# State-space outputs parked in one transfer a block, tokens in the order 8t+m, and a replanned order of work

## The chip, the cores and the metric

The kernel runs on one core of a Trainium2 chip. A core has engines that run on their own and meet at semaphores: TensorE (PE in the profile) multiplies matrices into PSUM, VectorE (DVE) and ScalarE (ACT) work on SBUF and PSUM, GpSimd (POOL) on SBUF, and SyncE (SP) issues most of the transfers. The metric is device time in microseconds, the median over runs; the kernel before has 750.5 us (three runs, 749.81 to 752.56).

## The reference

Two branches over the same 2048 tokens of 512 channels are mixed by a gate of the token:

```python
g = sigmoid((x * gate_w).sum(-1, keepdims=True))
a = softmax_attention(x, wqkv, 32 heads of 16) @ wo       # full 2048 x 2048 scores
# state-space branch, channel d, 128 complex states n:
K = einsum("dn,dnl,dn->dl", C, exp(dt * A * l), dt * B).real   # a filter of 2048 taps
b = causal_convolution(u, K).astype(bf16) + u * Dskip
out = g * a + (1 - g) * b
```

The attention has 32 heads with scores of 2048 by 2048 each, so 134 million exponentials. The state-space branch first makes the filters K from powers of complex numbers, then convolves each channel with its own filter.

## The kernel before, in words

**Attention.** The scores come in 2048 tiles. A tile is 128 keys by 512 queries of one head; four tiles (one for each 32-row strip of PE's array) make a quad, sixteen quads (all keys) a block, and there are 32 blocks, ordered by query chunk, then by heads. Tiles are put into groups of three (683 groups), each with a bank set SC0 or SC1 in PSUM by turns. For group g, PE computes the scores (`qk`, line 757 by way of the helper `mm`), ACT takes the exponential into a ring of tiles (`ex`, line 1018), and later PE multiplies the ring's tiles with the values (`pv`) into OA. The ring has NS = 14 tiles (named ET in the profile), from group NSG = 335 on NS2 = 24 (the rest is named EX).

**Sets.** ACT is relieved by DVE: in some groups ACT does only two tiles, and DVE turns the third into the bits of an exponential (`bits`, line 1040, tile DZ). Four such tiles, one of each strip, make a set; POOL makes three shifted copies of a set (`batch`, line 1059, tile DU), and PE adds all four to OA (`sums`). `decide` forms the sets as it hands out the tiles. A set begins only if fewer sets exist than the curve PACE allows at this group (`due`), only in certain key tiles of a block (DVK, and STRX, STRE, STRK for the last three), not within four groups of the last set, and if DVE has a reserve in the plan. WIN gives the number of buffers: two DZ and four DU up to group 560, then four and six.

**State-space branch.** `bases` and `tables` make powers on DVE (buffers Z, B16, T), `kstage` contracts them on PE into MB and writes filters to memory, `yloads` brings filters (H) and shifted inputs (U), `ystage` convolves on PE (MB) and multiplies with 1-g (gt) on DVE into Yst (line 1593). `yout` (line 1601) parks Yst in memory, four transfers a block of 32 channels, and loads it back with tokens on partitions (Yl, Yl2; line 1612). `outs` projects the attention with Wo, adds Yl and stores rows (fo).

**Gate.** `gate` (line 1620) makes the logits on PE, turns them by a trip through memory (gld to gp), takes an exponential on ACT (line 1638), three small DVE steps, and spreads g and 1-g by 14 small transfers (gt, gq).

**The order of the work** is written by a planner at build time. Each helper thread yields pieces with an engine and an estimated cost; between two groups, `Sched.fill` issues those that can start before a time limit (t+OVER), by earliest start and priority. `Prog` keeps a model clock of each engine. Each engine runs its queue strictly in that order, so a piece that waits holds back all behind it. If a group would lack matmul work (FILL up to group 260, then LOW), filler matmuls on a zero tile (wm) are added. DVE and POOL steps that would share a port are kept apart by waits (`locks`). SBUF addresses follow from each buffer's first and last use (`place`), and a buffer that takes over another's bytes waits for its users.

Of the kernel before, what the change touches and what calls it, by code (L numbers as in the profile page):

```python
# [56 lines left out]
NS = 14  # L57
NS2 = 24
NSG = 335
# [7 lines left out]
YLP = 4.5  # L67
YQ = 0
XGO = 'g14'
YGO = 'projs'  # L70
YLGO = 'K15'
BG0 = 'g0'
BG1 = 'g0'
BG2 = 'K4'
BG3 = 'g0'
TP = 2
KP = 0.4
NB = 2
NT = 2
TB = 0  # L80
# [4 lines left out]
HS = [4, 48, 8]  # L85
BACK = 0.4
# [17 lines left out]
DVCAP = 6  # L104
DVK = 14
JS = ((2, 0, 3, 1), (1, 0, 2, 3), (0, 2, 1, 3))
DVL = 16
STRX = 480
# [3 lines left out]
VG = 4 * VW + 16  # L112
ONES = struct.unpack("<f", bytes.fromhex("803f803f"))[0]
# [285 lines left out]
class Sched:  # L399
# [101 lines left out]
    def fill(self, until, pe_until, want=0):  # L501
        while True:
            best = None
            for t in self.thr:
# [3 lines left out]
                if t.eng == "PE":  # L508
# [7 lines left out]
                    if e + t.cost + room > pe_until and t.up > 0 or e > min(until, pe_until):  # L516
                        continue
# [35 lines left out]
def declare(nc, es):  # L553
# [188 lines left out]
def record(nc, p, B, ins):  # L742
# [106 lines left out]
    def proj_ev(kind, idx, c, bank):  # L849
        b, off, sl = bank  # L850
        if kind == "K":
            o, at, ky = KT, idx * S + 512 * c, (idx, c)
        elif c + idx:
            o, at, ky = B["Qs"], idx % 2 * 512, idx % 2
        else:
            o, at, ky = B["Q"], 0, 0
        op("DVE", lambda v: v.tensor_copy(o(at, [[1, 512]]), b(off, [[1, 512]])), [(b, sl, ('p', kind, idx, c))],
           [(o, ky)], c=.62)
# [11 lines left out]
    def mk_qm(b, j):  # L870
# [363 lines left out]
    def fp(qr, k, dims, off=0):  # L1234
        return B[f"Z{qr % NZ}"].f32(ZF.get(k[0], 0) + 128 * k[1] + off, dims)

    def fk(qr, *ks):
        return [(B[f"Z{qr % NZ}"], k, qr) for k in ks]

    PS = 2048  # L1240

    def weights(qr):

        Z = B[f"Z{qr % NZ}"]
# [109 lines left out]
    def zpart(qr):  # L1354

        Z = B[f"Z{qr % NZ}"]
# [43 lines left out]
    def ploads():  # L1400
        yield ("AFTER", "pd")
        for qr, go in enumerate((BG0, BG1, BG2, BG3)):
            Z = B[f"Z{qr % NZ}"]
# [11 lines left out]
    def bases():  # L1415
        for qr, go in enumerate((BG0, BG1, BG2, BG3)):
            yield ("AFTER", go)
            B16 = B[f"B16{qr % NB}"]
# [121 lines left out]
    def yloads():  # L1540
        yield ("AFTER", YGO)
        for v in range(2 * NBLK):
# [4 lines left out]
            for i in range(UN4):  # L1547
# [3 lines left out]
                    [(xs, (v // 8, s0)) for s0 in range(0, T, 4)], [(U, i, v)], c=.62, lat=3.5, b=UB * 2 / UN4, pace=True)  # L1551
            for q in range(4):
# [5 lines left out]
                for i in range(HN):  # L1558
# [3 lines left out]
                        [(kd, (u // 8, u // 2 % 4))], [(H, i, u)], c=.6, lat=3.5, b=HB / HN, pace=True)  # L1562
# [38 lines left out]
    def yout(blk):  # L1601
        w = blk % 2
        for j in range(4):
            yield ("SP", .6)
            dma("SP", lambda e, j=j: e.dma_start(yd.dram(512 * blk + 128 * j, [[8192, 2 * T], [8192 * 2 * T, R8], [1, 128]]),
                                                 Yst(1024 * w, [[128, R8], [1, 128]], 32 * j, 2 * T)),
                [(Yst, (w, h), blk) for h in range(2)], [(yd, (blk, j))], c=.6, lat=3.5, b=YB)
        yield ("AFTER", YLGO)
        for k, y in enumerate((Yl, Yl2)):
            yield ("SP", .6, YLP)  # L1610
            n = 128 >> k
            dma("SP", lambda e, k=k, y=y, n=n: e.dma_start(y(4 * n * blk, [[n, 4], [1, n]]), yd.dram(512 * blk + 8192 * k, [[8192 * 2, P], [128, 4], [1, n]])),
                [(yd, (blk, j)) for j in range(4)], [(y, blk)], c=.6, lat=3, b=.5, pace=True)
# [5 lines left out]
    def gate():  # L1619
# [16 lines left out]
        dma("SP", lambda e: e.dma_start(gp(0, [[1, 16]]), B["gld"].dram(0, [[16, P], [1, 16]])), [(B["gld"], c) for c in range(4)], key("gp"), c=.6, lat=2.5)  # L1636
# [10 lines left out]
        for j in range(4):  # L1647
            yield ("SP", .6)
            dma("SP", lambda e, j=j: e.dma_start(alt("gt", [[16, R8], [1, 16]], 32 * j), B["gd"].dram(0, [[16, T], [16 * T, R8], [1, 16]])),
                [(B["gd"], 0)], [(B["gt"], j)], c=.6, lat=2.5)  # L1650
            yield ("SP", .6)
            dma("SP", lambda e, j=j: e.dma_start(alt("gt", [[16, R8], [1, 8]], 32 * j + 1), B["gd"].dram(8, [[16, T], [16 * T, R8], [1, 8]])),
# [25 lines left out]
    def out_dma(lt, q="SP"):  # L1678
        dma(q, lambda e: e.dma_start(dap(ins["out"], 128 * lt * D, [[D, P], [1, D]]), fo((lt % 4) * D, [[1, D]])),
# [121 lines left out]
    def norms():  # L1801
        for b in range(31):
# [84 lines left out]
    op("DVE", lambda v: v.tensor_scalar(Qm(0, [[1, 512]]), OA(0, [[1, 512]]), msk(0, [[1, 1]]), None, ALU.mult),  # L1887
# [25 lines left out]
    for g in range(NG):  # L1913
# [114 lines left out]
```

## Time and profile before

| | us |
|---|---|
| median of the three runs | 750.5 |
| the profiled execution, its own time | 751.56 |
| span, first to last instruction | 749.8 |
| ACT busy | 729.4 |
| PE busy | 688.2 |
| DVE busy | 661.7 |
| POOL busy | 368.3 |

The profile is of one execution. A busy share is an average over stages that differ: before about 200 us DVE makes projections and filter parameters and takes no score tiles; from 200 to 630 us sets, filters and convolutions run side by side; after that the sets and the output projection. A row of the profile names the line, engine, operation, tiles and shapes, then the count, busy time and mean time, then the idle time of the engine just before and who ended it. Lines of helpers (757 for all matmuls, 1112 for many DVE steps) are told apart by their tiles.

### The profile page before, as it was taken

The page shows a single profiled execution, that of the slowest core. Times are in us where ns is not written, and L with a number is a line of the kernel's source. Part 1 is how long each engine was busy: PE and PEld are TensorE (multiplying, and loading weights), DVE is VectorE, ACT ScalarE, POOL GpSimd, SP SyncE. Part 2 cuts the span into 40 slices and gives each one's busy share as a digit, 9 for nine tenths or more (in the row PEclk, how much of TensorE's full clock was granted, in tenths as well). Part 3 has the DMA queues.
Part 4 walks back from the last instruction along what each step waited for, and adds up shares of the span by engine and source line. Part 5 has one row for each costly group of instructions (what it writes and reads, how often), then busy time and mean ns, then how long its engine had stood idle before and what let it go on. Part 6 is the DMA issues. An engine that isn't in the chain of part 4 may idle for free.

```text
span 749.8 us, 31499 instructions
## 1 busy us (share of the span) xinstructions
PE 688.2 (92%) x13936; PEld 290.6 (39%) x13936; DVE 661.7 (88%) x1113; ACT 729.4 (97%) x696; POOL 368.3 (49%) x368
## 2 busy tenths in 40 slices
PE   8777777888899999999999999999999999999997
PEld 4222232443434344434454344544444443222222
DVE  7999899999889888988989879999888888898876
ACT  7999999999999999999999989999999999999996
POOL 3000000000056777564453645467788788878763
PEclk9999999999999999999999999999999999999999
DMA  9858920221556457767268787737577774100000
GB/s 218 164 149 145 164 49 6 60 51 64 126 137 173 118 138 171 200 156 206 58 153 216 173 231 210 190 79 166 155 171 165 173 167 84 30 18 20 26 23 29
DMA packets 176588, 94.33 MB, mean 126 GB/s; under 512 B 116802, under 2 KB 159940, under 8 KB 176452
## 3 DMA queue, kind: packets, MB, share of 16 engines
q1 hardware_dynamic: 175492, 91.48, 50.8%
q8 instruction: 109, 1.79, 1.0%
q10 hardware_dynamic: 960, 0.85, 0.4%
q14 instruction: 27, 0.22, 0.1%
HBM read 63.42 MB, written 18.90 MB: 110 GB/s over the span
## 4 chain that ended last, share of the span: by engine, by line
ACT 77%; PE 17%; DVE 3%; DMA 1%; POOL 1%; issue 0%; DVEq 0%; SPq 0%; POOLq 0%
ACT ET L1018 63%; ACT EX L1018 14%; PE OA L757 7%; PE SC L757 7%; PE MB L757 3%; DVE DZ L1040 1%; POOL DU L1059 1%; DVE ft L1112 1%; DMA gp<-gm_gld 1%; DMA H<-gm_kd 0%; DVE T L1112 0%; DVE OT L1080 0%; DVE Yst L1593 0%; DVE OnT L1104 0%; DVE Qm L1887 0%
## 5 line engine op out<-in xcount | busy, mean ns | idle before, releaser
L1018 ACT ACTIVATE ET<-SC 128x1024 bf16<-128x1024 f32 (+1 forms) x538 | 590.0, 1348 | 8.0 <-PE SC L757 6.4
L1059 POOL INT64_ADD DU<-DZ x348 | 360.9, 1051 | 367.4 <-DVE DZ L1040 251.3
L1040 DVE TENSOR_SCALAR DZ<-SC 128x512 uint16<-128x512 f32 x468 | 312.7, 683 | 59.6 <-PE SC L757 47.9
L757 PE MATMUL SC<-Qm,KT 32*128 32x512 bf16 x2048 | 275.9, 385 | 47.9 <-ACT ET L1018 41.5
L757 PEld LDWEIGHTS SC<-Qm,KT 32*128 32x128 bf16 x2048 | 70.8, 91 | 251.3 <-ACT ET L1018 170.7
L1018 ACT ACTIVATE EX<-SC 128x1024 bf16<-128x1024 f32 (+1 forms) x145 | 148.3, 1236 | 0.7 <-PE SC L757 0.6
L757 PE MATMUL OA<-DU,VE 128*32 128x512 bf16 x1404 | 133.8, 387 | 3.0 <-POOL DU L1059 3.0
L757 PE MATMUL OA<-ET,VE 128*32 128x512 bf16 x1276 | 131.0, 389 | 0.3 <-ACT ET L1018 0.2
L757 PEld LDWEIGHTS MB<-U,H 128*32 128x32 bf16 x4096 | 83.9, 144 | 27.9 <-issue 18.3
L757 PE MATMUL MB<-U,H 128*32 128x128 bf16 (+7 forms) x4096 | 91.6, 225 | 1.3 <-DMA H<-gm_kd 1.0
L757 PE MATMUL OA<-wm 128*32 128x256 bf16 (+3 forms) x317 | 60.0, 344 | 1.2 <-DVE idf L812 1.2
L1112 DVE TENSOR_TENSOR T<-B,DT 128x1536 bf16<-128x1536 bf16 x64 | 60.6, 974 | 0.1
L757 PEld LDWEIGHTS OA<-DU,VE 128*32 128x32 bf16 x1404 | 36.5, 96 | 50.8 <-issue 35.9
L757 PEld LDWEIGHTS OA<-ET,VE 128*32 128x32 bf16 x1276 | 33.5, 95 | 48.9 <-issue 46.7
L757 PEld LDWEIGHTS MB<-T,Z 128*32 128x32 bf16 x2048 | 43.5, 155 | 10.7 <-issue 7.2
L757 PE MATMUL MB<-T,Z 128*32 128x64 bf16 (+1 forms) x2048 | 46.7, 235 | 0.0
L757 PE MATMUL OA<-DZ,VE 128*32 128x512 bf16 x468 | 46.5, 387 | 0.0
L757 PE MATMUL OA<-EX,VE 128*32 128x512 bf16 x304 | 42.8, 388 | 0.0
L1112 DVE TENSOR_TENSOR ft<-Z 128x512 f32<-128x512 f32 (+3 forms) x48 | 39.8, 855 | 0.1
L1112 DVE TENSOR_TENSOR Z<-ft,ft 128x1024 bf16<-128x1024 bf16 (+3 forms) x56 | 32.2, 574 | 0.5
L1080 DVE STREAM_TRANSPOSE OT<-OA 128x512 f32<-128x512 f32 x32 | 22.9, 716 | 2.1 <-PE OA L757 1.9
L1593 DVE TENSOR_TENSOR Yst<-MB,gt 128x512 bf16<-128x512 f32 x32 | 21.8, 682 | 3.3 <-PE MB L757 3.1
(141 smaller groups left out, 416.7 us busy)
## 6 DMA issues: line engine op xcount, KB each, us to landing
H<-gm_kd SPq DMA_DIRECT2D x128, 256.0 KB, 4.1
U<-gm_xs SPq DMA_DIRECT2D x128, 134.2 KB, 3.9
T<-B SPq DMA_DIRECT2D x16, 256.0 KB, 2.7
gm_yd<-Yst SPq DMA_DIRECT2D x64, 64.0 KB, 3.5
gm_kd<-Ks SPq DMA_DIRECT2D x64, 40.0 KB, 1.9
gm_xs<-xP SPq DMA_DIRECT2D x16, 136.0 KB, 5.7
gm_pd<-L SPq DMA_DIRECT2D x8, 256.0 KB, 4.1
Z<-gm_pd SPq DMA_DIRECT2D x8, 256.0 KB, 3.6
```

The lines of the kernel that those rows point to most:

```text
L757: op("PE", lambda t: t.matmul(out(), lhsT(), rhs(), start=start, stop=stop, skip_group_check=True, **kw), R, W, c=c, lat=.15, a=a, cfg=cfg)
L1018: op("ACT", lambda a: a.activation(E(at, [[1, 512 * n]]), sc(0, [[1, 512 * n]]), AF.Exp, scale=DH ** -0.5), [(sc, i, g) for i in range(n)] ...
L1040: op("DVE", lambda v: v.tensor_scalar(z.u16(512 * k, [[1, 512]]), sc(1024, [[1, 512]]), XS, XB, ALU.mult, ALU.add), [(sc, 2, g)], [(z, k, ...
L1059: op("POOL", lambda v, u=u, cut=cut: v.int64_add(u.u64(), z.u64(), cut * 0x0001000100010001), R, [(u, 0, i)], c=1.016, lat=.09, lk=True)
L1080: op("DVE", lambda v: v.transpose(OT(512 * w, [[1, 512]]), OA(0, [[1, 512]])), [(OA, 0, b)], [(OT, w, b)], c=.64)
L1112: op(eng, lambda v: v.tensor_tensor(o(), a(), b_(), f), R, W, c=c)
L1593: op("DVE", lambda v, w=w, h=h: v.tensor_tensor(Yst(1024 * w + 4 * h, [[128, R8], [8, 16], [1, 4]]), MB(0, [[1, R8], [R8, 16], [NC, 4]]), ...
```

## The change: what it does

- *Parking.* `yout` writes a block's Yst in one transfer (partition rows of 1024 elements, 2 KB runs) in place of four (runs of 128 elements, 256 bytes). The load back reads runs of 128 or 64 elements, for Yl in place of one run of 512.
- *Token order.* For this, the tokens of a tile of 128 stand in the order 8t+m (t of 16, m of 8) for token t+16m: the query copies read PSUM with steps of 16 (ROWS, TURNED), the gate's small transfers and the output rows follow the same order.
- *Buffers by quarter.* Z, B16 and T have a name for each quarter of the channels, so that `place` can give them bytes of their own; the flags that release a quarter stay (they use NZ, NB). A quarter's first tables no longer wait for those of the quarter before.
- *Ring.* NS 14 to 20, and 24 tiles from group 395 in place of 335.
- *Gate.* The exponential comes after group 100 (GATE).
- *Sets.* A set may begin only if the last set in its DZ buffer has been through POOL in the plan (`room`); four DZ and six DU buffers from group 480; another PACE curve; last key tiles of a block allowed from group 460.
- *Plan.* Other priorities, costs, start points, limits (OVER by whether the next group is a set's), filler and rest parameters.

The diff, cut:

```diff
-LAZY = 9
-PDEL = 0.3
+LAZY = 5
+PDEL = 0.43
...
-OUTP = 6
-YSEG = 4
+OUTP = 3.78
+YSEG = 2
...
-FILL = 1500
-LOW = 1300
-SURP = 256
+FILL = 1450
+LOW = 1200
+SURP = 192
...
-OVER = 0.5
-REST = (14, 0, 1792, 425)
+OVER = (0.27, 0.64)
+REST = (13, 1, 1792, 425)
...
-NS = 14
+NS = 20
...
-NSG = 335
+NSG = 395
...
-WIN = ((0, 560, 2, 4), (560, 679, 4, 6))
-PACE = ((0, 0), (40, 0), (90, 0), (140, 0), (200, 15.0), (270, 28.3), (340, 39.5), (420, 53.9), (500, 73.9), (570, 90.7), (630, 105.7), (683, 118.95))
+WIN = ((0, 480, 2, 4), (480, 679, 4, 6))
+PACE = ((0, 0), (61, 0), (78, 0.0), (149, 0.0), (206, 12.77), (270, 23.66), (340, 38.94), (414, 52.88), (500, 77.45), (564, 96.69), (630, 111.83), (683, 119.39))
...
-YLGO = 'K15'
-BG0 = 'g0'
-BG1 = 'g0'
-BG2 = 'K4'
-BG3 = 'g0'
-TP = 2
-KP = 0.4
+YLGO = 'K14'
+GATE = 'g100'
+BG0 = 'g25'
+BG1 = 'g20'
+BG2 = 'K3'
+BG3 = 'K3'
+TP = 0.86
+KP = 0.85
...
-HS = [4, 48, 8]
-BACK = 0.4
+HS = [4, 44, 8]
+BACK = 0.66
...
-DVCAP = 6
+DVCAP = 8.7
...
+FREE = 'u{}.2'
...
-STRX = 480
+STRX = 460
...
+ROWS = [[P, 4], [R8, T], [1, R8]]
+TURNED = [[P, 4], [1, T], [T, R8]]
...
-                    if e + t.cost + room > pe_until and t.up > 0 or e > min(until, pe_until):
+                    if e + t.cost + room > pe_until and (t.up > 0 or e > until) or e > pe_until:
...
-    for k in range(NB):
-        sb(f"B16{k}", 2 * 128 * 16)
-    for k in range(NZ):
-        sb(f"Z{k}", 2 * 128 * 32)
-    for k in range(NT):
-        sb(f"T{k}", 14 * 16 * CB)
+    for q in range(4):
+        sb(f"B16{q}", 2 * 128 * 16)
+        sb(f"Z{q}", 2 * 128 * 32)
+        for k in range(NT):
+            sb(f"T{q}{k}", 14 * 16 * CB)
...
-        op("DVE", lambda v: v.tensor_copy(o(at, [[1, 512]]), b(off, [[1, 512]])), [(b, sl, ('p', kind, idx, c))],
+        to, fr = ([[1, 512]],) * 2 if kind == "K" else (ROWS, TURNED)
+        op("DVE", lambda v: v.tensor_copy(o(at, to), b(off, fr)), [(b, sl, ('p', kind, idx, c))],
...
+    def room(w):
+        n = sum(st["w"] == w for st in sets)
+        old = [i for i, st in enumerate(sets) if st["r"] == f"{w}{n % WIN[w][2]}"]
+        return not old or FREE.format(old[-1]) in sch.flag
+
     def win(x):
-        return next((w for w, (lo, hi, *_) in enumerate(WIN) if lo <= x < hi and x >= plan["x"] + 4 and len(sets) < due(x)), None)
+        return next((w for w, (lo, hi, *_) in enumerate(WIN) if lo <= x < hi and x >= plan["x"] + 4 and len(sets) < due(x) and room(w)), None)
...
-                old = [k for k in range(blk) if tbuf(k) == tbuf(blk)]
+                old = [k for k in range(4 * qr, blk) if tbuf(k) == tbuf(blk)]
...
-        for j in range(4):
-            yield ("SP", .6)
-            dma("SP", lambda e, j=j: e.dma_start(yd.dram(512 * blk + 128 * j, [[8192, 2 * T], [8192 * 2 * T, R8], [1, 128]]),
-                                                 Yst(1024 * w, [[128, R8], [1, 128]], 32 * j, 2 * T)),
-                [(Yst, (w, h), blk) for h in range(2)], [(yd, (blk, j))], c=.6, lat=3.5, b=YB)
+        yield ("SP", .6)
+        dma("SP", lambda e: e.dma_start(yd.dram(P * 1024 * blk, [[1024, P // 2], [512 * P, 2], [1, 1024]]), Yst(1024 * w, [[1, 1024]])),
+            [(Yst, (w, h), blk) for h in range(2)], [(yd, blk)], c=.66, lat=3.5, b=2 * YB)
...
-            dma("SP", lambda e, k=k, y=y, n=n: e.dma_start(y(4 * n * blk, [[n, 4], [1, n]]), yd.dram(512 * blk + 8192 * k, [[8192 * 2, P], [128, 4], [1, n]])),
-                [(yd, (blk, j)) for j in range(4)], [(y, blk)], c=.6, lat=3, b=.5, pace=True)
+            dma("SP", lambda e, k=k, y=y, n=n: e.dma_start(y(4 * n * blk, [[n, 4], [1, n]]), yd.dram(P * 1024 * blk + 512 * P * k, [[P, P], [P * P, 4], [1, n]])),
+                [(yd, blk)], [(y, blk)], c=.6, lat=3, b=.55, pace=True)
...
+        yield ("AFTER", GATE)
         yield ("ACT", .3)
...
-        dma(q, lambda e: e.dma_start(dap(ins["out"], 128 * lt * D, [[D, P], [1, D]]), fo((lt % 4) * D, [[1, D]])),
+        dma(q, lambda e: e.dma_start(dap(ins["out"], 128 * lt * D, [[D, T], [T * D, R8], [1, D]]), fo((lt % 4) * D, [[1, D]])),
...
-        sch.fill(t, t + OVER, want)
+        over = OVER[0 if g + 1 in vec else 1]
+        sch.fill(t, t + over, want)
```

Further constants of the planner change in the same way (transfer costs, and the start points of the input rows).

More of the change, by code (lines that the diff above doesn't have):

```diff
@@ L1234, in fp @@
     def fp(qr, k, dims, off=0):
-        return B[f"Z{qr % NZ}"].f32(ZF.get(k[0], 0) + 128 * k[1] + off, dims)
+        return B[f"Z{qr}"].f32(ZF.get(k[0], 0) + 128 * k[1] + off, dims)
     def fk(qr, *ks):
-        return [(B[f"Z{qr % NZ}"], k, qr) for k in ks]
+        return [(B[f"Z{qr}"], k, qr) for k in ks]
     PS = 2048
     def weights(qr):
-        Z = B[f"Z{qr % NZ}"]
+        Z = B[f"Z{qr}"]
         e8, l8 = PS, 4096
@@ L1354, in zpart @@
     def zpart(qr):
-        Z = B[f"Z{qr % NZ}"]
+        Z = B[f"Z{qr}"]
         H10 = dv(1024, 2)
@@ L1402, in ploads @@
         for qr, go in enumerate((BG0, BG1, BG2, BG3)):
-            Z = B[f"Z{qr % NZ}"]
+            Z = B[f"Z{qr}"]
             yield ("AFTER", go)
@@ L1417, in bases @@
             yield ("AFTER", go)
-            B16 = B[f"B16{qr % NB}"]
+            B16 = B[f"B16{qr}"]
             if qr >= NB:
@@ L1428, in tables @@
         for qr in range(4):
-            B16 = B[f"B16{qr % NB}"]
+            B16 = B[f"B16{qr}"]
             yield ("AFTER", f"ba{qr}")
@@ L1550, in yloads @@
                                                                xs.dram((v // 2 * 32 + v % 2 * 4) * UW + 2 * UP * i + R8 - 1, [[D * UW, T], [-1, R8], [1, UN]])),
-                    [(xs, (v // 8, s0)) for s0 in range(0, T, 4)], [(U, i, v)], c=.62, lat=3.5, b=UB * 2 / UN4, pace=True)
+                    [(xs, (v // 8, s0)) for s0 in range(0, T, 4)], [(U, i, v)], c=.72, lat=3.5, b=UB * 2 / UN4, pace=True)
             for q in range(4):
@@ L1635, in gate @@
         yield ("SP", .6)
-        dma("SP", lambda e: e.dma_start(gp(0, [[1, 16]]), B["gld"].dram(0, [[16, P], [1, 16]])), [(B["gld"], c) for c in range(4)], key("gp"), c=.6, lat=2.5)
+        dma("SP", lambda e: e.dma_start(gp(0, [[1, 16]]), B["gld"].dram(0, [[16, T], [16 * T, R8], [1, 16]])), [(B["gld"], c) for c in range(4)], key("gp"), c=.6, lat=2.5)
+        yield ("AFTER", GATE)
         yield ("ACT", .3)
@@ L1886, in record @@
     par_mm("AreT", mb)
-    op("DVE", lambda v: v.tensor_scalar(Qm(0, [[1, 512]]), OA(0, [[1, 512]]), msk(0, [[1, 1]]), None, ALU.mult),
+    op("DVE", lambda v: v.tensor_scalar(Qm(0, ROWS), OA(0, TURNED), msk(0, [[1, 1]]), None, ALU.mult),
        [(OA, 0, ('p', "Q", 0, 0)), (msk, 0)], [(Qm, (0, j), 0) for j in range(4)], c=.68)
@@ L1951, in record @@
             want = max(want, REST[2])
-        sch.fill(t, t + OVER, want)
+        over = OVER[0 if g + 1 in vec else 1]
+        sch.fill(t, t + over, want)
         lack = want - p.act
         p.act = bare = 0
-        while lack >= 256 and p.tm["PE"] < t + OVER and g < NG - 1:
+        while lack >= 256 and p.tm["PE"] < t + over and g < NG - 1:
             z = zbank()
@@ L1991, in record @@
     for (i, eng, at, n), (f, o, W) in zip(ends, tail):
-        dma("ACT" if eng == "ACT" and i == 3 or i == 2 else "SP", lambda e, i=i, f=f, o=o, at=at, n=n: e.dma_start(dap(ins["out"], 128 * (12 + i) * D + at, [[D, P], [1, n]]), f(o, [[1, n]])),
+        dma("ACT" if eng == "ACT" and i == 3 or i == 2 else "SP", lambda e, i=i, f=f, o=o, at=at, n=n: e.dma_start(dap(ins["out"], 128 * (12 + i) * D + at, [[D, T], [T * D, R8], [1, n]]), f(o, [[1, n]])),
             W, [(B["d_out"], (12 + i, at))], c=.5, lat=2)
```

22 lines of the change are left out of this document (11 added, 11 removed).

## The prediction

> **What bounds the kernel now.** First the page: busy shares, then the chain that ended last.
>
> ```profile
> core 0 of [0], span 749.8 us
> PE 688.2 (92%) x13936; PEld 290.6 (39%) x13936; DVE 661.7 (88%) x1113; ACT 729.4 (97%) x696; POOL 368.3 (49%) x368
> ACT 77%; PE 17%; DVE 3%; DMA 1%; POOL 1%; issue 0%; DVEq 0%; SPq 0%; POOLq 0%
> L1059 POOL INT64_ADD DU<-DZ x348 | 360.9, 1051 | 367.4 <-DVE DZ L1040 251.3
> L1040 DVE TENSOR_SCALAR DZ<-SC 128x512 uint16<-128x512 f32 x468 | 312.7, 683 | 59.6 <-PE SC L757 47.9
> ```
>
> ACT sets the end: 97% busy and 77% of the chain. Its work is the softmax exponential: 2048 tiles of scores in 683 groups of three. Next, three pieces of the chain in order of time (start, length, instructions):
>
> ```profile
> 13.83 67.17 ACT ET L1018 x50
> 642.33 4.58 ACT EX L1018 x5
> 646.91 6.42 ACT ET L1018 x7
> ```
>
> The first piece holds groups of three tiles, 67.17/50 = 1.343 us each. Late in the span DVE takes the third tile (line 1040) and ACT does two: (4.58+6.42)/12 = 0.917 us. So a tile on DVE spares ACT 0.426 us. DVE takes them in sets of four: 468/4 = 117 sets, 1.71 us each.
>
> So the time can move in two ways: by the number of sets, and by ACT's idle time. For the second, the busy time of the engines by stage (columns: stage, PE, PEld, DVE, ACT, POOL, clock, DMA share, GB/s):
>
> ```profile
> 81.00:90.00 9.00, 6.48 (x125) 2.83 (x121) 5.86 (x18) 7.28 (x7) 0.00 (x0) 0.85 1.18 181
> 150.00:216.00 66.00, 57.33 (x1352) 26.82 (x1352) 61.13 (x111) 66.00 (x54) 3.90 (x4) 1.00 0.30 76
> 216.00:250.00 34.00, 32.48 (x623) 13.15 (x615) 30.25 (x52) 32.18 (x35) 26.24 (x26) 1.00 0.67 174
> 250.00:290.00 40.00, 38.09 (x794) 16.61 (x790) 35.22 (x59) 38.50 (x41) 28.55 (x29) 1.00 0.56 138
> 290.00:360.00 70.00, 65.90 (x1520) 31.23 (x1512) 62.54 (x96) 69.99 (x69) 39.58 (x38) 1.00 0.70 182
> 360.00:430.00 70.00, 66.39 (x1666) 33.45 (x1659) 63.54 (x109) 69.94 (x67) 36.32 (x34) 1.00 0.62 151
> 430.00:500.00 70.00, 65.83 (x1563) 32.41 (x1563) 60.79 (x98) 67.60 (x66) 36.64 (x36) 0.98 0.72 192
> 500.00:560.00 60.00, 59.40 (x1269) 27.76 (x1266) 54.25 (x89) 59.02 (x64) 45.55 (x45) 1.00 0.59 147
> 560.00:600.00 40.00, 39.31 (x796) 17.23 (x790) 32.98 (x54) 38.88 (x43) 32.40 (x33) 1.00 0.76 175
> 600.00:700.00 100.00, 99.20 (x1419) 29.64 (x1411) 85.33 (x133) 100.00 (x111) 83.94 (x83) 1.00 0.27 61
> ```
>
> ACT is idle 9.00-7.28 = 1.72 in the first row, then 0, 1.82, 1.50, 0.01, 0.06, 2.40, 0.98, 1.12 and 0: 9.6 us. That is what a new order can win from ACT's idle time; head and tail of the span keep their instructions.
>
> **What the idle time waited for.** The timeline of ACT, and of PE at the same places, gives:
>
> ```profile
> 85.17 0.22 ACT L1638 ACTIVATE ge<-gp 128x16 f32<-128x16 f32 x1 [1.50 <-DMA gp<-gm_gld]
> 89.63 128.43 ACT L1018 ACTIVATE ET<-SC 128x1536 bf16<-128x1536 f32 x99 [0.22 <-PE OA L757]
> 244.61 0.40 PE L757 MATMUL OA<-DU,VE 128*32 128x512 bf16 x4 [0.59 <-POOL DU L1059]
> 245.38 14.82 ACT L1018 ACTIVATE ET<-SC 128x1024 bf16<-128x1024 f32 x15 [0.64 <-PE SC L757]
> 431.09 0.67 PE L757 MATMUL MB<-U,H 128*32 128x128 bf16 x32 [0.77 <-DMA H<-gm_kd]
> 432.83 2.87 ACT L1018 ACTIVATE ET<-SC 128x1024 bf16<-128x1024 f32 x3 [1.02 <-PE SC L757]
> 594.60 0.40 PE L757 MATMUL OA<-DU,VE 128*32 128x512 bf16 x4 [0.48 <-POOL DU L1059]
> 595.36 2.85 ACT L1018 ACTIVATE ET<-SC 128x1024 bf16<-128x1024 f32 x3 [0.61 <-PE SC L757]
> DVE DZ L1040 <- POOL DU L1059: 6.8, 11, 1.2
> ```
>
> Three kinds are visible. The gate's exponential sits in ACT's queue before its data has landed. PE, in order, waits for a POOL sum of a set, and the next scores come late; DVE waits for POOL too, because its set buffer is still being read. And PE waits for a filter load.
>
> **The change, part by part.**
>
> *Gate after group 100.* Groups 0 to 56 precede 89.63, so group 100 begins at 89.63+43*1.343 = 147.4. Its input landed by 85.2, so the 1.50 goes, and with it the 0.22 of the restart: -1.72. Three DVE steps and 14 small transfers on SP move with it, from a stretch with DMA share 1.18 to one with 0.30. Consumers:
>
> ```profile
> L1652 SPq DMA_DIRECT2D gt<-gm_gd x4: 601/601/1160, 93.8 to 98.2; - x4
> L1593 DVE TENSOR_TENSOR Yst<-MB,gt x32: 651/681/693, 235.4 to 627.3; 128x512 bf16<-128x512 f32 x32
> ```
>
> The last gate load is issued 13 us after the exponential, so near 162; its first reader is at 235.4. Cover of 70 us; bound 0 to -1.72, and I take all of it.
>
> *Sets.* Before, the curve allows 53.9 sets at group 420. A set takes four groups (0.25 a group); where a block's last three key tiles are barred (outside groups 480 to 640), five sets take 64 tiles, 0.234 a group. So 53.9+60*0.234+160*0.25+39*0.234 = 117.1, and the trace has 117. After: 52.88 at group 414, tiles barred only to 460: 52.88+46*0.234+180*0.25+39*0.234 = 117.8, below the curve's 118.8 at 679. Half a set, -0.85; bounds +1.71 (116, if the new rule that a set buffer be free delays some) and -3.42 (119).
>
> *Stalls of 216 to 290.* The curve there falls from 0.25 to 0.224 sets a group (groups 149 to 206) and from 0.19 to 0.17 (to 270); the exponential ring grows from 14 to 20 tiles, so PE can lag further; the buffer rule keeps DVE from starting into a buffer POOL still reads. Of 3.32 I take half, -1.66 (0 to -3.32). (At the paces above, groups 149 to 206 lie near 213 to 268 us.) What is cut comes back at groups 270 to 340, near 333 to 405 us (0.16 to 0.218 a group), where two rows lose 0.07 in 140 us. At the idle rate of 216 to 290, 3.32 in 74, those 72 us would lose 3.2; I take a quarter, +0.80, as the density stays under the 0.25 of that stretch.
>
> *430 to 500.* The filter wait and its aftermath, 2.40. The parked outputs ease the SP queue:
>
> ```profile
> Yl<-gm_yd SPq DMA_DIRECT2D x16, 128.0 KB, 3.0
> L1605 SPq DMA_DIRECT2D gm_yd<-Yst x64: 316/462/1844, 251.7 to 632.4; - x64
> L1612 SPq DMA_DIRECT2D Yl<-gm_yd x32: 348/503/1226, 570.1 to 637.3; - x32
> ```
>
> 48 issues of 0.462 us, 22 us of SP's 380, go; filter loads behind them start up to 3*0.462 = 1.4 us sooner, against a wait of 0.77. Half, -1.20 (0 to -2.40), as the new order can expose another load.
>
> *500 to 600.* Density cannot fall here. The buffer rule may end the POOL wait at 595: -0.60 (+1.0, about what the row 500 to 560 loses now, to -2.10).
>
> *At nothing.* The query copy reads PSUM in steps of 16. Rows with a stepped and a plain read agree:
>
> ```profile
> L857 DVE CAST Qs<-MB 128x512 bf16<-128x512 f32 x15 | 10.3, 685 | 1.1 <-PE MB L757 1.0
> L1630 DVE COPY gl<-MB 128x512 f32<-128x512 f32 x1 | 0.7, 691 | 0.1
> ```
>
> 15 copies and the first masked query: +0.01 each at most by these rows, and only the last is on the chain. Output rows leave in another order, same bytes and run length. The Yl load now gathers 256-byte runs instead of 1 KB; nothing reads Yl until the output stage:
>
> ```profile
> L1717 DVE SCALAR_TENSOR_TENSOR fo<-MB,g,Yl x8: 730/740/750, 643.6 to 700.4; 128x512 bf16<-128x512 f32 x8
> ```
>
> The last load, issued at 637.3, may take 6.3 us before that reader waits; it took 3. If that cover went, the output stage would start later behind a PE that is 99% busy from 600 on. The Trainium skill (DMA: Bandwidth & Descriptors, the table ahead of its parts) puts line rate at runs of 512 bytes or more, which speaks against this load; taken as a doubling, an estimate, the load would take 6 us, and the sum would be the same with 0.3 us of cover left. No run here shows it.
>
> *Sum:* -1.72-0.85-1.66+0.80-1.20-0.60 = -5.23. The profiled execution took 751.56 (span 749.8 and 1.76 around it): 746.33. The median of the runs, 750.5, is 1.06 below it: **745.3**. All best ends: -1.72-3.42-3.32-2.40-2.10 = -12.96, 737.5. All worst: +1.71+3.2+1.0 = +5.9, 756.4.
>
> **The rivals.** A difference of about 0.5%, 3.75 us, is what a measurement here can tell from none; faster means below 746.75, slower above 754.25.
>
> *B, the stalls only move.* Each wait comes from a fixed order meeting real durations; a new order brings other waits. For: waits of one kind appear at places far apart (244, 594). Only the gate counts: 750.5-1.72 = 748.8.
>
> *C, the plan is clean.* The named stalls shrink to a fifth and a set more fits: -1.72-0.8*(1.82+1.50+2.40+0.98+1.12)-1.71 = -9.7, 740.8. For: 600 to 739 runs with no idle time at full density. Against: POOL and DVE block each other most where state-space work and sets mix, and that mix stays.
>
> *D, sets starve (slower).* Up to group 480 there are two set buffers. A set's scores take four groups, 3.7 us, and its three POOL sums 3*1.051 = 3.2 us, more with POOL's waits; two sets at full density take 8*0.917 = 7.3 us. So "buffer free" may come a group or more late each time, at 414 to 480 where the plan now runs without reserve. At 9 groups for two sets, 66*(0.25-0.222) = 1.8 sets are lost. Gate, stalls and loads bring 4.38 without the set term; D decides from 4.38/1.71 = 2.6 lost sets. Five lost, if DVE's reserve binds too, cost 8.55: 750.5+8.55-4.38 = 754.7. Against: DVE waits for a buffer only 11 times now, 1.2 us at most, so buffers mostly come free in time.
>
> *E, the clock.* Filler matmuls are trimmed (1500 to 1450, 1300 to 1200).
>
> ```profile
> 62.50:75.00 12.50, 9.70 (x158) 3.13 (x155) 12.22 (x19) 12.50 (x10) 0.00 (x0) 1.00 0.88 163
> 86.78 0.39 PE L757 MATMUL SC<-Qm,KT 32*128 32x512 bf16 x1 [2.11 <-ACT ET L1018]
> 88.00:89.00 1.00, 1.00 (x27) 0.36 (x23) 0.42 (x2) 1.00 (x2) 0.00 (x0) 0.50 1.35 140
> 436.00:438.00 2.00, 1.27 (x30) 0.45 (x22) 2.00 (x4) 1.99 (x3) 2.00 (x2) 1.00 0.94 280
> 440.00:442.00 2.00, 2.00 (x23) 0.42 (x19) 0.39 (x1) 1.94 (x2) 1.34 (x2) 0.50 0.64 197
> ```
>
> PE at 78% busy keeps the full clock; twice it is granted half, once after PE stood 2.11 us at 86.78, once after a stretch at 64%. A trim of 3 to 8% leaves 71% or more. If it dropped all the same, each spell costs ACT about what 430 to 500 lost less the filter wait, 1.4 us; six of them with only the gate won are 750.5-1.72+8.4 = 757.2. The Trainium skill (TensorE: Matmul & The Clock Gate, Part 1) lets the clock halve only after an idle window of some 3.4 us; by that rule E would have no chance. The trace differs: the idle stretch ahead of the first spell was 2.11 us, and the clock halved.
>
> **How the numbers follow.** Forecast 0.50 (own range 741.5 to 749), B 0.22, C 0.13, D 0.10, E 0.05. Faster: 0.40 of the forecast, all of C, 0.04 of B: 0.57. Slower: most of D and E: 0.13. Same: 0.30. Range 740 to 753.5: it leaves out the better part of C's lower side and the upper halves of D and E, under 0.2.
>
> **What would show it.** Right: no ACT wait for gp; DZ count 468 or 472; fewer than 11 waits of DVE on POOL; ACT idle in the stages above near 5 us. Wrong: DZ at 456 or below (D); more half-clock spells (E); ACT idle still 8 us (B). The prediction fails if the sets change by more than two.

## The result and the profile after

The kernel after takes 744.92 us, the median of six runs (743.8 to 747.07). Six runs of the kernel before, beside them, have a median of 751.70 (749.81 to 753.5). The ratio is 0.9914, with an interval from 0.9891 to 0.9937: faster by 4.7 to 8.2 us. The profiled execution of after took 746.18 us with a span of 744.3, against 751.56 and 749.8 before: its span is 5.5 us shorter. Two executions that took far longer than all others of their kernel (1283.66 us, the profiled one of the first gate run below, and 2827.87 us, one of the kernel before) count in no ratio.

The page of after, busy shares and the chain that ended last:

```profile
core 0 of [0], span 744.3 us
PE 692.2 (93%) x14173; PEld 299.0 (40%) x14173; DVE 659.3 (89%) x1109; ACT 728.8 (98%) x696; POOL 362.1 (49%) x365
ACT 91%; PE 8%; DVE 0%; issue 0%; DVEq 0%
L1049 DVE TENSOR_SCALAR DZ<-SC 128x512 uint16<-128x512 f32 x464 | 310.6, 685 | 58.9 <-PE SC L760 54.9
```

ACT still sets the end, and more purely: 91% of the chain in place of 77%. DVE takes 464 tiles in place of 468, so there are 116 sets, one fewer and not half a set more. By the prediction's price that gives ACT 1.71 us more to do, though its busy time is 728.8 us against 729.4; more on that below. The time was won elsewhere, and the busy time by stage shows where (columns: stage, PE, PEld, DVE, ACT, POOL, clock, DMA share, GB/s):

```profile
81.00:90.00 9.00, 6.52 (x181) 3.02 (x177) 8.63 (x25) 9.00 (x8) 0.00 (x0) 1.00 1.17 153
216.00:250.00 34.00, 33.01 (x757) 15.98 (x758) 31.55 (x54) 34.00 (x36) 21.64 (x21) 1.00 0.63 164
250.00:290.00 40.00, 38.19 (x888) 18.17 (x880) 37.88 (x57) 40.00 (x40) 21.00 (x21) 1.00 0.67 182
290.00:360.00 70.00, 66.83 (x1551) 32.95 (x1549) 61.81 (x108) 69.72 (x70) 40.16 (x39) 1.00 0.40 105
360.00:430.00 70.00, 67.21 (x1599) 34.17 (x1595) 65.01 (x103) 70.00 (x68) 38.57 (x38) 1.00 0.84 219
430.00:500.00 70.00, 67.78 (x1520) 32.33 (x1521) 56.31 (x89) 67.31 (x68) 43.17 (x42) 0.98 0.59 145
500.00:560.00 60.00, 59.36 (x1286) 27.83 (x1283) 49.70 (x81) 60.00 (x65) 46.99 (x46) 1.00 0.70 177
560.00:600.00 40.00, 39.51 (x780) 16.91 (x777) 33.35 (x52) 40.00 (x45) 33.23 (x34) 1.00 0.73 180
```

Stage length less ACT's busy time is its idle time: 0, 0, 0, 0.28, 0, 2.69, 0 and 0, with nothing in the two stages left out. That is 2.97 us in place of 9.61, so 6.64 less. The waits, from the view that names them, and ACT's timeline where it still stands:

```profile
DVE DZ L1049 <- POOL DU L1068: 1.8, 3, 0.6
ACT ET L1027 <- PE SC L760: 4.0, 6, 1.7
17.34 130.41 ACT L1027 ACTIVATE ET<-SC 128x1536 bf16<-128x1536 f32 x97 [0.53 <-PE SC L760]
147.44 0.41 ACT L1646 ACTIVATE ge<-gp 128x16 f32<-128x16 f32 x1
432.49 1.94 ACT L1027 ACTIVATE ET<-SC 128x1024 bf16<-128x1024 f32 x2 [1.68 <-PE SC L760]
434.99 1.02 ACT L1027 ACTIVATE ET<-SC 128x1024 bf16<-128x1024 f32 x1 [0.56 <-PE SC L760]
734.09 1.40 ACT L1027 ACTIVATE ET<-SC 128x1024 bf16<-128x1024 f32 x1
739.22 0.59 ACT L1999 CAST fo<-MB 128x512 bf16<-128x512 f32 x1 [3.72 <-PE MB L760]
```

The gate's exponential starts at 147.44 without a wait. DVE waits for POOL three times instead of eleven. One large stall is left, at 430 to 436.

The difference of the two spans, piece by piece: idle time in the stages -6.64; one wait at 17 us +0.53; one set fewer +1.71. The first exponential starts 0.31 later (10.83 against 10.52). The tail, from the last exponential's end (734.09 + 1.40 = 735.49) to the end of the span, is 8.8 us against 7.9, +0.9. These make -3.2. About -2.3 is left, and it lies in ACT's busy time, which should be 1.71 longer and is 0.6 shorter. An exponential in a run overlaps the next one, and one that stands alone between two waits doesn't: the lone group at 434.99 takes 1.02 us where a group in a run takes 0.917. The waits of ACT's exponentials before were these, and one more for gp:

```profile
ACT ET L1018 <- PE SC L757: 6.4, 14, 1.0
ACT ET L1018 <- PE OA L757: 1.1, 4, 0.4
ACT EX L1018 <- PE SC L757: 0.6, 2, 0.4
```

That is 21 times, against 6 after; 15 waits at 0.1 make an estimate of 1.5. Taken from the starts of the exponentials in the two traces, a group of two tiles before a wait lasts 0.16 to 0.17 us longer than one in a run, the wait itself left out. At that price 15 waits make 2.5, so nothing large stays open.

### The profile page after: what moved, and what is told of

It is laid out like the page before. It is cut to its first block, busy times and chain, and to the rows that moved or that the text cites. A ratio compares the mean times of both kernels' runs of the same rounds, so it can differ in the third digit from the quotient of the medians.

```text
span 744.3 us, 31873 instructions
## 1 busy us (share of the span) xinstructions
PE 692.2 (93%) x14173; PEld 299.0 (40%) x14173; DVE 659.3 (89%) x1109; ACT 728.8 (98%) x696; POOL 362.1 (49%) x365
## 4 chain that ended last, share of the span: by engine, by line
ACT 91%; PE 8%; DVE 0%; issue 0%; DVEq 0%
ACT ET L1027 86%; ACT EX L1027 5%; PE SC L760 3%; PE OA L760 3%; PE MB L760 2%; DVE Qm L1895 0%; DVE VE L870 0%; DVE fo L1996 0%; DVEq L722 0%; DVE wm L814 0%; DVE KT L1898 0%; ACT ge L1646 0%; DVE idf L815 0%; DVEq L386 0%
## 5 line engine op out<-in xcount | busy, mean ns | idle before, releaser
L1027 ACT ACTIVATE ET<-SC 128x1024 bf16<-128x1024 f32 (+1 forms) x636 | 684.5, 1335 | 4.2 <-PE SC L760 4.0
L1068 POOL INT64_ADD DU<-DZ x345 | 354.6, 1042 | 344.5 <-PE MB L760 184.9
L760 PE MATMUL SC<-Qm,KT 32*128 32x512 bf16 x2048 | 272.8, 386 | 10.6 <-ACT ET L1027 6.2
L760 PE MATMUL OA<-ET,VE 128*32 128x512 bf16 x1489 | 155.0, 389 | 30.6 <-ACT ET L1027 29.4
L760 PEld LDWEIGHTS MB<-U,H 128*32 128x32 bf16 x4096 | 91.3, 143 | 32.2 <-issue 15.6
L760 PE MATMUL MB<-U,H 128*32 128x128 bf16 (+7 forms) x4096 | 97.4, 224 | 2.0 <-issue 1.9
L760 PEld LDWEIGHTS OA<-ET,VE 128*32 128x32 bf16 x1489 | 40.0, 95 | 98.1 <-ACT ET L1027 54.1
L760 PE MATMUL OA<-wm 128*32 128x256 bf16 (+3 forms) x550 | 75.1, 343 | 1.2 <-DVE idf L815 1.2
L1027 ACT ACTIVATE EX<-SC 128x1024 bf16<-128x1024 f32 (+1 forms) x47 | 51.0, 1219 | 0.0
L760 PEld LDWEIGHTS OA<-wm 128*32 128x32 bf16 (+2 forms) x550 | 20.8, 96 | 10.3 <-issue 7.0
```

Source lines behind the costliest of these rows:

```text
L760: op("PE", lambda t: t.matmul(out(), lhsT(), rhs(), start=start, stop=stop, skip_group_check=True, **kw), R, W, c=c, lat=.15, a=a, cfg=cfg)
L1027: op("ACT", lambda a: a.activation(E(at, [[1, 512 * n]]), sc(0, [[1, 512 * n]]), AF.Exp, scale=DH ** -0.5), [(sc, i, g) for i in range(n)] ...
L1068: op("POOL", lambda v, u=u, cut=cut: v.int64_add(u.u64(), z.u64(), cut * 0x0001000100010001), R, [(u, 0, i)], c=1.016, lat=.09, lk=True)
```

## The experiments

The theory after the result: the gain is ACT's idle time, and the buffer rule and the new curve took it away, by keeping sets from being formed faster than POOL clears them. Three rivals: the gate and the parking did it; the roomier buffers did it; or any new order would have drawn other waits and this draw was a lucky one. Each ratio below is to the kernel before.

**The gate alone.** The order of before on every engine, with only the gate's exponential and its followers moved (the edit in words):

```diff
+ entries that write ge, gp (POOL/DVE step), g, g1: behind the exponential of group 100
+ gd, gg: behind group 102; gt: behind 106; gq: behind 110
```

It ran twice.

> The kernel before, with every engine's order kept, but the gate's exponential and what follows from it (three DVE steps, 14 transfers) moved behind group 100. My theory (ACT's idle time is the currency): the wait of 1.50 us for gp and the restart of 0.22 us go, ACT idle falls from 9.6 to about 7.9 us, and the time falls by 1.7 us, near 749. Rival (the stalls only move): the 1.7 us come back at a later wait, the time stays within 0.5 us of the kernel before.

> The kernel before with its order on every engine, only the gate's exponential and what follows it moved behind group 100. The theory that the gate is worth its whole wait: the wait for gp (1.50 us and 0.22 of restart) is gone from the profile, nothing new stands in its place, and the time is 1.7 us below before (ratio 0.998). Rival, a move only lets a later wait grow: the wait for gp is gone, ACT's idle time in the stages from 216 us on grows by 1 us or more, and the ratio is 1.000.

Measured: ratio 0.9983 (0.9961 to 1.0004), then 1.0004 (0.9984 to 1.0024). The mean, 0.9993, is 0.5 us with some 1.1 to either side, so 1.7 lies just outside. The profile of the second run shows why, in the stage of the gate and in waits of DVE, PE and ACT:

```profile
81.00:90.00 9.00, 7.55 (x200) 3.31 (x196) 8.73 (x20) 9.00 (x8) 0.00 (x0) 1.00 1.04 173
DVE gp L1661 <- ACT ge L1657: 1.3, 1, 1.3
PE MB L776 <- DVE Qs L876: 1.4, 3, 0.7
152.56 64.50 ACT L1037 ACTIVATE ET<-SC 128x1536 bf16<-128x1536 f32 x51 [0.21 <-PE OA L776]
```

The 1.72 at the gate is gone. But DVE reaches the moved gate steps early and stands 1.3 us for the exponential. Its next copies come late, PE waits for one of them (Qs) at 150.8, and then ACT for PE. Compare when the same group's exponential starts in the two traces, less the difference at the first group: the lead over before is 1.8 us at group 60, 0.5 at group 112, and 0.1 at group 198, near 260 us. So most of the win is lost within 15 us behind the new place. In after DVE doesn't wait there: its first gate step starts at 148.08, and the exponential has ended at 147.85. This run therefore doesn't measure what the gate is worth in after; it shows that the place of the DVE steps decides it.

Later waits move too. PE now waits for a filter at 412. The filter's load, before first, is issued 0.8 us later there and lands 1.75 us later (412.36 against 410.61), while PE comes to it 0.3 earlier:

```profile
406.90 3.15 SPq L1561 DMA_DIRECT2D H<-gm_kd  x3
407.70 2.83 SPq L1580 DMA_DIRECT2D H<-gm_kd  x3
412.40 0.67 PE L776 MATMUL MB<-U,H 128*32 128x128 bf16 x32 [0.94 <-DMA H<-gm_kd]
```

ACT loses 1.22 us in that stage where it had lost 0.06, and 0.9 less in the next. Over all ten stages its idle time falls from 9.61 to 8.89, by 0.7: the stages behind the gate lose 1.0 more than before. That is the rival's direction and its ratio of 1.000, though only 0.64 of the 1.0 lies from 216 us on, where it asked for 1 or more.

**Parking and token order alone.** The order of before, with one transfer where the fourth stood, and the layout of after:

```diff
-        for j in range(4): gm_yd<-Yst, 32 rows, runs of 128 elements
+        gm_yd<-Yst, whole block, runs of 1024 elements
...
+ROWS, TURNED, and the transposed patterns of the gate's transfers and the output rows
```

> The kernel before with the order of every engine kept, but the outputs parked in one transfer a block (placed where the fourth of the four stood) and tokens in the order 8t+m. Theory of the prediction: SP's queue is relieved of 48 issues (22 us), the filter wait near 430 us shrinks, gain 0 to 1.2 us. Rival (parking does nothing by itself): ACT idle stays at 9 to 10 us and the time within 0.5 us. Rival from the other side: the load back in runs of 256 bytes is slow and the output stage waits; then ACT's end stays but the tail grows by 1 us or more.

Measured: 749.8 us (ten runs), ratio 0.9976 (0.9952 to 1.0000), so 1.8 us with 1.8 to either side. The stage with the filter wait and that wait, of this kernel:

```profile
430.00:500.00 70.00, 66.28 (x1598) 32.92 (x1586) 61.65 (x99) 68.21 (x68) 37.63 (x37) 0.98 0.65 177
PE MB L760 <- DMA H<-gm_kd: 0.4, 1, 0.4
DVE DZ L1044 <- POOL DU L1063: 6.3, 10, 1.2
```

The idle time there falls from 2.40 to 1.79 and PE's wait for filters from 1.0 to 0.4: in this profile fewer transfers on SP bring the filters sooner, as the theory says. The tail is 8.2 us against 7.9, so the load back in 256-byte runs doesn't hold up the output stage. The other stages stay within 0.05 of before, and DVE's waits for POOL stay: those belong to the order, not to the layout.

**A new order for no reason.** The planner's delay changed by 0.01, in before and in after:

```diff
-PDEL = 0.3
+PDEL = 0.31
...
-PDEL = 0.43
+PDEL = 0.44
```

> The kernel before, replanned by a change of no meaning: PDEL, the reserve that the planner keeps for POOL, from 0.30 to 0.31. It measures what replanning alone does. Theory (the gain has causes): ACT idle stays near 9.6 us, with the gate's 1.7 among it, and the time within 1.5 us of 750.5. Rival (a plan is a draw of lots): ACT idle moves by 3 us or more either way, so that a gain of 6 us needs no cause but a lucky plan.

> The changed kernel, replanned by a change of no meaning: PDEL from 0.43 to 0.44; the count of tiles on DVE stays 464. In the kernel before such a step cost 3 us (754.75, ACT idle 4 us more), all of it behind 287 us where the orders part. Theory (causes): ACT idle stays within 2 us of the changed kernel's 3.5 and the time within 2 us of 744.9. Rival (the constants were drawn for their luck): the time rises by 3 us or more, to 748 or above, by new waits at new places.

Measured: before with 0.31 takes 754.75, ratio 1.0047 (1.0021 to 1.0073); after with 0.44 takes 747.43, ratio 0.9968 (0.9943 to 0.9993). The numbers of tiles on DVE are unchanged, 468 and 464. In the first, ACT's idle time in the ten stages is 13.5 us, 3.9 more than before, so the rival of the first text came out. Its longest wait, PE's stands without a cause that the profile shows (the longest of them ends just ahead of that wait), and DVE's waits for POOL:

```profile
461.12 2.13 ACT L1018 ACTIVATE EX<-SC 128x1024 bf16<-128x1024 f32 x2 [1.73 <-PE SC L757]
PE MB L757 <- issue: 3.1, 4, 1.9
DVE DZ L1040 <- POOL DU L1059: 8.6, 13, 1.2
```

So a plan drawn anew, with nothing else changed, moves the ratio by 0.0047 (from 1) and by 0.0054 (from 0.9914), some 3.5 and 4 us. The second is less certain: its profile has 2.6 us of idle time in the ten stages, no more than after, and its 747.43 lies between the theory's 2 us and the rival's 748. Executions of one kernel also differ in the clock that PE was granted; those with a mean of 0.999 or 1.0 take 744.79 to 746.69 us here and 743.8 to 744.18 in after. This is what the size of any single term must be read against. Both these plans with the new rules stay ahead of both plans without them.

**The buffer rule off**, once alone (472 tiles on DVE) and once with the end of the curve lowered so that the sets are again 116:

```diff
-        return not old or FREE.format(old[-1]) in sch.flag
+        return True
...
-(630, 111.83), (683, 119.39)
+(630, 108.5), (683, 116.6)
```

> The changed kernel without the rule that a set's buffer be free in the plan (it replans; the count of tiles on DVE becomes 472 in place of 464, two sets more). Theory: two sets spare ACT 2*1.71 = 3.4 us, but DVE's waits for POOL's buffers come back (11 rather than 3) and with them 2 to 3 us of ACT idle: the time ends within 1.5 us of 744.9. Rival A (the rule costs more than it brings): 741.5. Rival B (the rule is the main cause of the gain): 748 or more.

> The changed kernel without the rule that a set's buffer be free, its curve cut at the end (group 630: 108.5, 683: 116.6) so that DVE takes 464 tiles as in the changed kernel. The run without the rule and with 472 tiles took 751.7; its tail was 12.1 us behind the last exponential in place of 8.8, with the output stage begun 26 us later, and it had 3.6 us more ACT idle time. If the two sets more are what hurt (PE has no room for their 24 quads and the output stage slips behind the end), the tail returns to 9 us and the time is 747 to 749. If the missing rule hurts (DVE waits for POOL's buffers), DVE has 9 or more such waits, ACT idle stays at 7 us, and the time stays near 750, since ACT has 3.4 us more to do.

Measured: 751.67, ratio 0.9997 (0.9971 to 1.0024), and 751.14, ratio 1.0005 (0.9984 to 1.0026). The whole gain is gone in both, with two sets more and with none more: rival B of the first text, and the missing rule in the second, though there the tail shrank to 8.4 us, as it should if the two sets more had hurt. DVE's wait for POOL in the second:

```profile
DVE DZ L1049 <- POOL DU L1068: 6.5, 11, 1.1
```

These are the waits of before again (6.8 us, 11 times), with everything else of the change in place. ACT's idle time in the ten stages is 6.35 and 6.31 us against 2.97. Executions with a mean clock of 0.999 or 1.0 take 748.84 to 750.9 us in these two kernels, above all of those named for after and its replan.

What the rule does to the waits shows in every plan. In the profiles of the kernels with it, here and below, DVE waits for POOL at most six times, 0 to 3.9 us in all; without it, the execution of 1283.66 us apart, 10 to 13 times, 6.3 to 8.6 us. What it does to the time is less sure. Taking it out costs 6 to 7 us here, of which some 4 could be the draw of the plan: the two curves part only behind group 564, so up to there these two kernels are one draw and not two. And a kernel with the rule can be slow all the same, as the next one and the last show. The rule is a likely cause; its size isn't shown.

**The old curve in after:**

```diff
-PACE = (... (149, 0.0), (206, 12.77), (270, 23.66), (340, 38.94), (414, 52.88), (500, 77.45), ...)
+PACE = (... (140, 0), (200, 15.0), (270, 28.3), (340, 39.5), (420, 53.9), (500, 73.9), ...)
```

> The changed kernel with the curve of the kernel before (0.25 sets a group from 140 to 200 in place of 0.224; 0.25 from 420); 464 tiles on DVE. Theory: the denser start brings ACT idle time back at 205 to 290 us, about 1.7 us of the 3.3 that went, time 746 to 747.5. Rival (density does not matter, the buffer rule and the ring do): no idle time there, within 1 us of 744.9.

Measured: 753.1, ratio 1.0025 (1.0008 to 1.0042), with 464 tiles as in after. Idle time at 216 to 290 is only 0.81, so the old curve doesn't bring the old stalls there back while the rule is on. Neither text's time came out. The loss lies behind: 4.94 from 360 to 600, and in the output stage. Output tiles and ACT's wait for the last of them, this kernel first, then after:

```profile
L1725 DVE SCALAR_TENSOR_TENSOR fo<-MB,g,Yl x8: 729/742/752, 657.4 to 715.7; 128x512 bf16<-128x512 f32 x8
L1729 DVE TENSOR_TENSOR fo<-MB,Yl x4: 675/686/691, 721.3 to 739.3; 128x512 bf16<-128x512 f32 x4
ACT fo L1999 <- remote: 7.1, 1, 7.1
```

```profile
L1725 DVE SCALAR_TENSOR_TENSOR fo<-MB,g,Yl x8: 710/742/753, 633.1 to 695.6; 128x512 bf16<-128x512 f32 x8
L1729 DVE TENSOR_TENSOR fo<-MB,Yl x4: 674/678/691, 700.3 to 728.8; 128x512 bf16<-128x512 f32 x4
```

The output stage begins 24 us later, and its last full tile comes at 739.3 where it came at 728.8. PE then still has output products to do after the last exponential: ACT waits 7.1 us for them where it waited 3.7, and the tail is 12.1 us where it was 8.8. The plan without the rule and with 472 tiles shows the same (first output tile 659.3, tail 12.07). So the curve also decides when the state-space work is done, and a late end of that can cost 3.3 us in the tail. It doesn't always: the second kernel without the rule begins its output stage as late (658.8), but its last full tiles come ahead of ACT's last exponential (740.9), and its tail is 8.4:

```profile
L1729 DVE TENSOR_TENSOR fo<-MB,Yl x4: 681/692/693, 720.5 to 734.3; 128x512 bf16<-128x512 f32 x4
```

**Ring and buffers.** A ring of 14 tiles as before; the same with Z, B16 and T shared between the quarters again (the order on every engine is then that of the ring of 14 alone, only addresses differ); and a ring of 12:

```diff
-NS = 20
-NSG = 395
+NS = 14        (12 in the last)
+NSG = 335
...
-B[f"Z{qr}"], B[f"B16{qr}"], B[f"T{blk // 4}{tbuf(blk)}"]
+B[f"Z{qr % NZ}"], B[f"B16{qr % NB}"], B[f"T{tbuf(blk)}"]      (second kernel)
```

> The changed kernel with the exponential's ring as before (14 tiles, 24 from group 335); 464 tiles on DVE. Theory: the ring of 20 lets PE lag and is part of why 216 to 290 us lost nothing; with 14, ACT idle in 200 to 430 us rises by 1 to 2 us, time 746 to 747. Rival (the ring does nothing for ACT): within 1 us of 744.9. Rival (lottery): 748 or more, with waits spread over the span.

> The kernel after with a ring of 14 tiles, 24 from group 335, and with Z, B16 and T shared between the quarters again, as before the change; the order of every engine is that of the run with the ring of 14 alone, only the addresses differ. If the buffers by quarter do nothing by themselves (they are written well ahead): the same time as the ring of 14, near 745.5 (ratio 0.990 to 0.993), and ACT idle 3 to 4 us. Rival, they take away waits of the first tables of a quarter: DVE waits for PE or DMA at Z, B16 or T by 1 us or more at a time, DZ tiles come late behind them, ACT is idle 5 us or more, and the time is 748 or above (ratio 0.996).

> The kernel after with a ring of 12 tiles (24 from group 335) and nothing else changed; the plan comes out with 468 score tiles on DVE, one set more than after. It tells the third DZ buffer from the smaller ring. If the ring's size does nothing: 743 to 746 (ratio 0.989 to 0.993). If 12 tiles bind: ACT or PE waits for the ring (exponentials waiting for PE OA, or PE for ACT at SC) grow by more than 3 us, and the time is 749 or above (ratio 0.998).

Measured: 745.52, ratio 0.9915 (0.9886 to 0.9945); 745.26, ratio 0.9932 (0.9911 to 0.9954); 749.69, ratio 0.9987 (0.9966 to 1.0008). Neither the larger ring nor the buffers by quarter gain anything that can be measured. They only make room that this plan doesn't need. A ring of 12 seems to bind, though it comes with a set more and is a new draw: ACT now waits for the ring, which shows as a wait for OA, where the ring's tiles are read:

```profile
ACT ET L1027 <- PE OA L760: 2.7, 6, 1.0
```

That is below the 3 us expected. The time came out as expected for a ring that binds, but the profiled execution is the fastest of the ten, 746.61 us, and doesn't show the rest.

**A third DZ buffer**, to let the rule pass more sets, with the ring of 12 to make room; its control is the ring of 12 above:

```diff
-WIN = ((0, 480, 2, 4), (480, 679, 4, 6))
+WIN = ((0, 480, 3, 4), (480, 679, 4, 6))
```

> The kernel after with a ring of 12 tiles (24 from group 335) and a third DZ buffer up to group 480: the rule that a buffer be free lets more sets begin, 472 score tiles on DVE in place of 464, so two sets more. If a set is worth 1.71 us and the rule keeps the waits away: -3.4 us, 741.5 (ratio 0.986), DVE waits for POOL 3 us at most. Rival, the plan without the rule showed that denser sets push the state-space work and the output stage back: the first output tile comes after 650 us, the tail between the last exponential and the end grows from 8.8 to 11 or 12 us, and the time is 746 to 750 (ratio 0.993 to 0.998).

Measured: 758.71, ratio 1.0125 (1.0075 to 1.0175), 9 us slower than its control, with one set more than it. Neither expectation held: the output stage came early (629.6) and the time lies above both. DVE never waits for POOL here. ACT's idle time in the ten stages is 19.4 us, 17.9 of it from 216 to 430. Two of its waits, and PE at the second:

```profile
266.97 20.54 ACT L1027 ACTIVATE ET<-SC 128x1024 bf16<-128x1024 f32 x21 [4.12 <-PE OA L760]
291.90 2.79 ACT L1027 ACTIVATE ET<-SC 128x1536 bf16<-128x1536 f32 x2 [4.39 <-PE OA L760]
289.23 0.40 PE L760 MATMUL OA<-DU,VE 128*32 128x512 bf16 x4 [1.31 <-POOL DU L1068]
290.25 0.40 PE L760 MATMUL OA<-DU,VE 128*32 128x512 bf16 x4 [0.61 <-POOL DU L1068]
291.47 0.40 PE L760 MATMUL OA<-ET,VE 128*32 128x512 bf16 x4 [0.82 <-DVE OT L1089]
```

Each is at the end of a block, where PE must add the block's last sets to OA before DVE may empty it (OT) and the next block may begin. POOL is behind there; PE waits for it twice, then for OT, and the ring fills meanwhile. So in this plan a third buffer moved the wait for POOL from DVE to PE, where it is dearer. That fewer sets in flight are what helps fits this, but wasn't tried by itself, nor was how much of the 9 us the small ring or the new draw adds.

## Why the prediction was right, and which of its steps were not

The forecast was 745.3, the median is 744.92; for the profiled execution 746.33 was worked out, and it took 746.18. The bound, ACT with idle time as the thing to win, was right. The terms were not as good as the sum: most were off, and that their errors cancelled is luck. Read at their places in the profile of after, the six are -1.72, +1.71, -3.32, +0.21, +0.29 and -2.10, together -4.93 where -5.23 was forecast. What the sum put at nothing came to about -0.5: head and tail and the wait at 17 us cost 1.8, and fewer waits shortened ACT's busy time by 2.3. That the median was met so closely is luck as well. The sum started from 750.5; the six runs of before beside after have 751.70, and against them after is faster by 4.7 to 8.2 us, with 5.2 forecast.

*Gate, -1.72.* In the profile of after the wait is gone as put down. What it is worth isn't shown: alone it brought 0.5 us with 1.1 to either side, but there DVE stood 1.3 us for the moved exponential, which it doesn't in after. The step costed the transfers that moved and their readers, not where DVE would stand when it reaches the moved steps.

*Sets, -0.85.* Wrong in sign: 116 sets, +1.71, the worst end of the range given. The step counted what the curve allows, and the rule binds: without it the planner forms 118.

*Stalls of 216 to 290, -1.66.* Undersized: all 3.32 went, the best end given. That the curve thins there was given as one reason, the ring as another, the rule as the third. The smaller ring changes the time by nothing that can be measured. With the old curve 0.81 is lost there and without the rule 1.17, so with either of the two most of it is gone; but then 5.0 and 5.2 are lost in the stages behind. What the two do isn't tied to that place.

*Density at 333 to 405, +0.80.* Two rows that lost 0.07 lose 0.28, +0.21. Density returned without the stalls. Without the rule these rows lose 2.87 and 1.67 in the two kernels above, so the price was right in kind, and the step had not counted the rule there.

*430 to 500, -1.20.* The filter wait went, and the parking alone shrank it in its one profile (2.40 to 1.79). But after loses 2.69 there, +0.29, to something new. PE at that place, and its clock:

```profile
431.62 0.49 PE L760 MATMUL MB<-U,H 128*32 128x104 bf16 x18 [1.93 <-issue]
432.00:434.00 2.00, 2.00 (x36) 0.82 (x34) 1.79 (x3) 1.51 (x2) 0.00 (x0) 0.65 0.84 247
434.00:436.00 2.00, 2.00 (x34) 0.56 (x26) 1.66 (x3) 1.44 (x2) 1.53 (x2) 0.50 0.17 43
```

PE stands 1.93 us for nothing that the profile shows. From 432.6 its clock is at half for 3.4 us. What held it is open. One thing recurs: in the raw traces this stand, the one of 1.9 us in before with 0.31 and one of 2.3 us in the kernel with the third DZ buffer each begin 0.4 to 0.6 us after a 16-KB transfer of the instruction queue that carries PE's program has started. Whether that holds PE was not tested.

*500 to 600, -0.60.* All 2.10 went, its best end.

*At nothing.* The Yl load in 256-byte runs took 3.1 us against 3.0: the rule of the Trainium skill (DMA: Bandwidth & Descriptors, the table ahead of its parts), taken as a doubling, is not borne out here. For the output rows the step was wrong. "Same bytes and run length" doesn't settle the price; the order of the rows counts, or the longer address pattern that it needs, which no run tells apart:

```profile
L1679 SPq DMA_DIRECT2D out_dram<-fo x12: 332/356/362, 644.3 to 728.4; - x12
out_dram<-fo SPq DMA_DIRECT2D x14, 128.0 KB, 1.7
```

```profile
L1687 SPq DMA_DIRECT2D out_dram<-fo x12: 538/544/597, 633.8 to 729.5; - x12
out_dram<-fo SPq DMA_DIRECT2D x14, 128.0 KB, 2.3
```

An issue takes 0.544 us in place of 0.356 (before first, then after), and the rows land 2.3 us after it in place of 1.7. The parking alone shows the same 0.545. Of the tail's 0.9 some 0.45 lies behind ACT's last issue (it ends at 741.69, 2.6 us before the end of the span, and ended at 747.64, 2.2 before); the other 0.45 is ACT's wait for the last products, 3.72 against 3.28.

*The rivals.* B (waits only move) is what a replan of before does, at +3.5 us; in after the waits shrank. C's mechanism, a clean plan, came true but for one stall, and its further set did not. D was right that the rule delays sets, and wrong that it costs: one set went, below its 2.6, and without the rule the gain was gone. E: filler products rose (550 where there were 317 of the kind that goes to OA), and the half-clock spell shown above followed a stand, not a trim; ahead of the tail there are two spells in each profile. That stand was 1.93 us, again shorter than the idle window of some 3.4 us of the Trainium skill (TensorE: Matmul & The Clock Gate, Part 1). The trace disagrees with that rule as before.

*What would show it.* Right: no wait for gp, three waits of DVE on POOL, idle time of 2.97 us where about 5 was named. Wrong: 468 or 472 tiles.

## What to carry to other kernels

When engines with fixed orders feed each other through few buffers, let the planner begin a unit only when its buffer is free in the plan: here that cut DVE's waits for POOL from ten or more to six or fewer in every plan, at the price of one or two sets. It didn't make every plan fast: with the old curve, and with a third buffer and a smaller ring, the kernel with the rule was slower than before. Before believing a gain of half a per cent from a change that replans, replan once for no reason: here that alone moved the time by some 4 us. A wait that is removed is worth its length only if no other engine must then wait at the new place, and if what comes next, with its loads, is ready that much earlier.

## What the runs showed of the hardware that was not expected

- An output transfer of the same size and run length takes half as long again to issue (0.544 against 0.356 us) when neighbouring partitions write rows that lie 16 rows apart; the order of the rows and the longer address pattern were not told apart.
- PE can stand for 1.93 us with nothing that the profile shows as its cause, and is then granted half its clock for 3.4 us though it is busy throughout.
- The time of one program goes with the granted clock. Ten executions of the parking alone lie between 747.68 us at a mean clock of 0.999 and 752.69 at 0.991: 5 us for 0.8% of clock, as large as the whole change. Ahead of the tail every spell at half clock in the traces of this case lasts 3.4 us, so 0.8% is three to four of them, some 1.4 us each, an estimate from these figures. Whether the spells cost the time or the stands ahead of them isn't told apart.
